# A new hand-written order for a retention and feed-forward kernel on one core: which engine does each step, when transfers are issued, and 42 waits between GpSimd and VectorE

## The chip, the core and the metric

The kernel runs on one core of a Trainium2 chip. The core has five engines with a queue each: TensorE (PE, matrix products), VectorE (DVE), ScalarE (ACT), GpSimd (POOL) and SyncE (SP), which here only issues transfers. Sixteen DMA engines serve the core. The metric is the device time of one execution in microseconds; lower is better. Every engine works through its own queue in order, and waits on semaphores for the others.

## What is computed

First a decayed attention for 8 batches of 8 heads over 576 positions of 64 numbers, then a feed-forward layer on all 4608 rows:

```python
Dmat = np.where(rel >= 0, gamma[:, None, None] ** rel[None, :, :], 0.0)   # rel[i, j] = i - j
ret = (scale * q @ k.T) * Dmat ; attn = ret @ v
x = attn.transpose(0, 2, 1, 3).reshape(4608, 512)
h = x @ w_in                    # 512 -> 2048
s = np.sin(alpha * h)
g = h + s * s / (alpha + 1e-09)
out = g @ w_out                 # 2048 -> 512
```

## The kernel before

The work is cut into nine groups of 512 rows. Groups 0 to 7 are the first 512 positions of a batch each, and group 8 holds the last 64 positions of all eight batches. Each small piece of work is a *step* with a name such as `PR.3.14.2`: a kind, the group or batch, and indices. The order of all steps is written out by hand in one long string, `STEPS`, with 1491 entries. At the end of the function a loop reads the entries from first to last and emits each as instructions; what stands earlier in the string stands earlier in the queue of its engine. An entry can say four things:

```
CA.3.q.1.2:G q16.3.1=12 <SQ.1.13
```

The step is the scaling of a raw block of q of batch 3; `:G` puts it on GpSimd (A is ScalarE, V VectorE, G GpSimd, P TensorE); `q16.3.1=12` places its result in the 12th of the buffers of that kind; `<SQ.1.13` makes it wait for the end of another step that it does not need any data from. Buffers are numbered slots: 8 banks of PSUM, 16 of 4 KB (`r4`), 28 of 2 KB (`h2`), 16 of 1 KB (`s1`). A step that writes a slot waits for those that still read it. There is no other scheduler.

The kinds of steps that the text speaks of, with the lines of the profile:

- LD (L431, L435): SyncE loads a raw block of q, k or v of 512 KB, two per tensor and batch, into an `r4` slot. LE does the same for the last 64 positions (L656). WI and WO load the weights from GpSimd's queue.
- CA (L458, copies of v L335): scales a raw block and converts it to 16 bits. XP (L490) turns blocks by a DMA transpose; for batches 0 and 1, TU (L476, TensorE) and TK (L335, copy) do.
- OU (L509), EV, TS (L335), MA (L534), MB (L537), NS (L542), ST (L548): the chain of the decayed k·v state. Of these only OU runs on TensorE.
- SC (L561, TensorE), MK (L574, VectorE): scores and their mask. VA, VB (L592) and SA (L628) apply them, KP copies the result into x.
- PR (L779, TensorE): a block of h in a PSUM bank. SI (L787, ScalarE): its sine. SQ (L797 on ScalarE, L798 on VectorE or GpSimd): the square. PD (L802, VectorE): g from square and bank, after which the bank is free.
- G2 (L818) multiplies g of group 0 by w_out; FI copies the result, OS stores it. Groups 1 to 8 use seven products instead of eight: TT (L854) forms differences of w_out once, SM (L866) sums and differences of g, PP (L886) the products on TensorE, CP (L335) copies and AD (L907) additions of results, OQ (L913, L914) the stores, mostly from SyncE's queue.
- KB (L422): products of zeros that keep TensorE busy while data is awaited at the start.

Two of the engines have a special relation in this kernel: the waits written with `<` stand on GpSimd steps only, each for a VectorE step beside it (35 of them before).

Of the kernel before, what the change touches and what calls it, by code (L numbers as in the profile page):

```python
# [34 lines left out]
KB.2.256.3; MA.0.2:V s32.0.2=17; RL.0.1:G; WI.1; TK.1.q.1.2:A qT.1.1=18; VB.0.1; MB.0.2:V; KB.8.256.7
ST.0.2:G <MB.0.2; ST.0.1:V; WI.3; SA.0.1; PR.0.2.0 hps.0.2=5; LD.1.k.1 raw.1.k.1=12; WO.0; KP.0.1.0:V; KP.0.1.1:A
KB.2.256.7; PR.0.2.1; CA.1.k.0.2:V k16.1.0=19; PR.0.0.2 hps.0.0=0; SI.0.2 s.0.2=0; LD.1.v.1 raw.1.v.1=13
CA.1.q.0.2:G q16.1.0=20; NS.0.3; PR.0.9.0 hps.0.9=1; PR.0.1.2 hps.0.1=2; SQ.0.2:V ss.0.2=1; PR.0.8.0 hps.0.8=3
SI.0.1 s.0.1=2; WO.1; PR.0.3.2 hps.0.3=4; SI.0.0 s.0.0=3; WO.2; PR.0.9.1; SQ.0.1:A ss.0.1=4; PR.0.11.2 hps.0.11=6
# [928 lines left out]
```

## Time and profile before

| | us |
|---|---|
| three runs | 300.96, 300.7, 303.81 |
| their median | 300.96 |
| the profiled execution | 300.28 |
| its span on the core | 298.4 |
| TensorE busy in it | 288.1 |

The profile is of one execution. Busy times are of its span, and the 1.9 us between span and time lie around it. Busy time of TensorE has modelled ends, so that short pauses between matmuls do not show as idle. The name L802 is line 802 of the kernel before; the changed kernel is one line shorter, so that the same line is L801 there. Names such as `r`, `h`, `s` and `g` in the rows are the buffers `r4`, `h2`, `s1` and `g16`.

### The profile page before, as it was taken

The numbers are of one execution on the slowest core, as the hardware profiler recorded it, in microseconds if no ns is written. First come the engines' busy times: TensorE is split into PE (matmuls) and PEld (weight loads), VectorE is DVE, ScalarE is ACT, GpSimd is POOL, SyncE is SP. The second block draws the span as 40 slices with busy tenths as digits, with TensorE's granted clock in tenths as the row PEclk, the third lists the DMA queues.
The fourth block names the chain that finished last, engine by engine and source line by source line (L and its number), as shares of the span: only waits on it lengthen the run. The fifth ranks groups of instructions, "written<-read, shape, count | busy, mean of one in ns | idle before, by whom it ended". The sixth has DMA issues, their size and how long they took to land.

```text
span 298.4 us, 8737 instructions
## 1 busy us (share of the span) xinstructions
PE 288.1 (97%) x3625; PEld 185.5 (62%) x3625; DVE 249.3 (84%) x369; ACT 191.2 (64%) x306; POOL 174.8 (59%) x161
## 2 busy tenths in 40 slices
PE   8999999998999999999999999999999999999994
PEld 4665445554666656667765667667665666465883
DVE  2567899999999899988989989879889766998931
ACT  1645952788756777597638864774677576877510
POOL 6745965389773865983794749974525543004380
PEclk9999999999999999999999999999999999999999
DMA  7999999999999999877977574167645000671054
GB/s 225 319 249 236 216 219 314 303 229 237 194 238 251 196 177 248 194 165 148 237 223 158 134 165 111 32 109 179 105 108 126 0 2 0 168 183 40 2 133 115
DMA packets 119511, 49.89 MB, mean 167 GB/s; under 512 B 69792, under 2 KB 118960, under 8 KB 119472
## 3 DMA queue, kind: packets, MB, share of 16 engines
...
## 4 chain that ended last, share of the span: by engine, by line
PE 73%; DVE 8%; DMA 6%; POOL 5%; SPq 4%; issue 2%; ACT 1%; DVEq 0%; ACTq 0%; POOLq 0%
PE banks L779 34%; PE banks L886 27%; DMA r<-in_q_dram 4%; DVE g L802 4%; PE banks L818 4%; SPq L435 4%; PE banks L561 2%; PE banks L592 2%; POOL s L798 2%; POOL r L866 2%; PE banks L509 1%; DMA r<-in_k_dram 1%; DVE h L574 1%; PE banks L628 1%; POOL h L458 1%
## 5 line engine op out<-in xcount | busy, mean ns | idle before, releaser
L779 PE MATMUL banks<-r,w_in 128*128 128x512 f16 (+1 forms) x608 | 139.1, 368 | 1.8 <-DVE g L802 1.3
L787 ACT ACTIVATE s<-banks,alpha 128x512 f16<-128x512 f32 x144 | 95.3, 686 | 55.0 <-PE banks L779 50.8
L802 DVE SCALAR_TENSOR_TENSOR g<-s,inva,banks 128x512 f16<-128x512 f16 x144 | 102.4, 741 | 15.9 <-ACT s L797 8.4
L779 PEld LDWEIGHTS <-w_in 128*128 128x128 f16 x608 | 57.6, 98 | 54.2 <-issue 3.2
L886 PEld LDWEIGHTS <-g 128*128 128x128 f16 x640 | 61.8, 98 | 17.1 <-issue 0.2
L797 ACT ACTIVATE s<-s 128x512 f16<-128x512 f16 x85 | 51.6, 628 | 1.4
L886 PE MATMUL banks<-w_out,g 128*128 128x256 f16 x384 | 51.2, 273 | 0.1
L458 POOL TENSOR_TENSOR h<-r,cn 128x1024 f16<-128x1024 f32 (+1 forms) x26 | 42.3, 1633 | 15.0 <-DVE s L798 5.9
L866 POOL TENSOR_TENSOR r<-g 128x1024 f16<-128x1024 f16 x10 | 21.6, 2162 | 37.0 <-DVE g L802 18.9
L798 POOL TENSOR_TENSOR s<-s 128x512 f16<-128x512 f16 x23 | 25.3, 1102 | 23.9 <-ACT s L787 19.8
L574 DVE TENSOR_TENSOR h<-banks,mask 128x1024 f16<-128x1024 f32 (+1 forms) x32 | 35.1, 1113 | 2.5 <-PE banks L561 2.4
L335 ACT COPY h<-banks 128x512 f32<-128x512 f32 (+2 forms) x32 | 20.8, 650 | 24.5 <-PE banks L886 17.8
L886 PE MATMUL banks<-r,g 128*128 128x256 f16 x256 | 34.8, 273 | 0.0
L886 PEld LDWEIGHTS <-r 128*128 128x128 f16 x256 | 24.5, 98 | 6.4 <-POOL r L866 0.5
L907 DVE TENSOR_TENSOR h<-banks,h 128x512 f32<-128x512 f32 (+1 forms) x26 | 16.7, 645 | 10.4 <-PE banks L886 8.2
L866 POOL TENSOR_TENSOR g<-g,r 128x1024 f16<-128x1024 f16 x8 | 17.4, 2183 | 12.6 <-DVE r L866 6.7
L335 ACT CAST r<-banks 128x1024 f16<-128x1024 f32 (+1 forms) x16 | 14.8, 932 | 10.7 <-PE banks L592 8.2
L798 DVE TENSOR_TENSOR s<-s 128x512 f16<-128x512 f16 x36 | 17.8, 499 | 4.3 <-ACT s L787 3.4
L458 DVE TENSOR_TENSOR h<-r,cn 128x512 f16<-128x512 f32 (+1 forms) x14 | 16.4, 1184 | 5.0 <-DMA r<-in_k_dram 4.2
L866 DVE TENSOR_TENSOR r<-g 128x1024 f16<-128x1024 f16 x22 | 16.6, 759 | 0.1
L886 PE MATMUL banks<-w_out,r 128*128 128x256 f16 x128 | 16.4, 273 | 0.0
L886 PE MATMUL banks<-r 128*128 128x256 f16 x128 | 16.2, 273 | 0.2 <-POOL r L866 0.2
...
## 6 DMA issues: line engine op xcount, KB each, us to landing
...
```

Of the source, the lines that this page charges most:

```text
L335: return eng.copy(d_, s_) if eng is nc.scalar else eng.tensor_copy(d_, s_)
L435: return eng.dma_start(t_, src[nm][b, :, 256 * p : 256 * p + 256, :].rearrange("h (i r) d -> i h (r d)", r=2))
L458: return eng.tensor_tensor(dst[:, a0:a1].rearrange("p a r t d -> p t (a r) d"), t_.rearrange("p (t a) x -> p t a x", t=2)[:, :, a0:a1].rea ...
L574: return nc.vector.tensor_tensor(ret(b, p, y).rearrange("p t (z x) -> p (t z) x", z=2)[:, :, 0:n], bank(f"sc.{b}.{p}.{y}", 2).rearrange("p ...
L779: i = matmul(bank(hps)[:, cols], w_in16[:, a, u * P : (u + 1) * P], x_of(n)[:, a, cols], start=starts(hps), stop=(a == KT - 1), skip_group ...
L787: return nc.scalar.activation(small(f"s.{name}")[:, cols], bank(f"hps.{name}")[:, cols], mybir.ActivationFunctionType.Sin, bias=0.0, scale ...
L797: return nc.scalar.activation(ss_t, s_t, mybir.ActivationFunctionType.Square)
L798: return eng.tensor_tensor(ss_t, s_t, s_t, MULT)
L802: return nc.vector.scalar_tensor_tensor(g_of(n)[:, u, cols], small(f"ss.{name}")[:, cols], inva[:, u : u + 1], bank(f"hps.{name}")[:, cols ...
L866: return eng.tensor_tensor(S[s], a, b, op)
L886: i = matmul(bank(f"{rows[c]}.{n}")[:, 256 * c : 256 * c + 256], left[:, 0, 128 * c : 128 * c + 128], right[:, 0, :], start=starts(f"{rows ...
L907: return nc.vector.tensor_tensor(x, bank(f"{b}.{n}")[:, cols], x, ADD)
```

## The change

The string `STEPS` is replaced by another with 1487 entries; no other line differs. The first nine entries are the same. The mix of steps is the same but for the warm-up products KB (19712 columns before, 20224 after) and a few steps that are cut or joined differently. Three things change: the order in every queue, the engine of about a hundred steps, and the waits with `<` (25 of the 35 are gone or changed, 32 are new or changed, 42 in all). Many slots change with them. The engines by kind, as ScalarE/VectorE/GpSimd:

| kind | before | after |
|---|---|---|
| SQ | 85/36/23 | 75/38/31 |
| CP | 22/10/0 | 27/5/0 |
| SM | 0/40/24 | 0/43/21 |
| CA | 12/14/33 | 14/15/30 |
| CE | 1/2/9 | 2/3/7 |
| MB | 0/6/16 | 0/4/18 |

In SyncE's queue the first fifteen loads keep their order; from then on single loads and transposes change places (LD.2.q.1 now ahead of LD.2.v.0, LD.3.k.1 ahead of LD.3.k.0), and the stores OQ of the second half are shuffled, with OQ.8.22, OQ.8.21 and the two halves of OQ.8.12 still the last. A few lines of the string, around the steps that the prediction speaks of (cut):

```diff
-LD.4.k.0 raw.4.k.0=10; SI.1.13 s.1.13=5; G2.0.2.1 op.0.2=3; CA.2.v.0.2:A v16.2.0=14; TT.4.1:V T4=12; G2.0.2.3
-SQ.1.13:V ss.1.13=6; LD.3.k.1 raw.3.k.1=11; SI.1.3 s.1.3=1; PD.1.13 gT.1=1; CA.3.q.1.2:G q16.3.1=12 <SQ.1.13; G2.0.0.2
...
-CA.2.k.1.0:G; G2.0.2.0; SI.1.7 s.1.7=7; FI.0.1:V osb.0.1=17; TT.4.0:V; PR.1.9.2 hps.1.9=5; SQ.1.7:A ss.1.7=3
...
+PR.1.3.2 hps.1.3=2; CA.2.v.0.2:V v16.2.0=14; G2.0.0.2; TT.4.1:V T4=12; SI.1.3 s.1.3=1; FI.0.1:V osb.0.1=17
+SQ.1.6:A ss.1.6=2; G2.0.2.1; LD.4.k.0 raw.4.k.0=10; CA.3.q.1.2:G q16.3.1=12; CA.2.v.1.2:A v16.2.1=15; PD.1.6 gT.1=1
...
+G2.0.0.3; SQ.1.5:V ss.1.5=10; SQ.1.7:A ss.1.7=3; CA.2.k.1.0:G <TT.4.0; PD.1.7; G2.0.2.0; FI.0.0:A osb.0.0=20
```

The first place is VectorE's queue in batch 1, before. The rows are, from the top, CA.2.q.1.2, TT.4.1, SQ.1.13, PD.1.13, PD.1.6, SQ.1.5, FI.0.1, TT.4.0, PD.1.7, PD.1.5, PD.1.3 and EV.2.0; the names are buffers, and the brackets hold the engines and transfers that are waited for.

```order
L458 TENSOR_TENSOR h_68<-r_67,cn 128x2x8x64 [waits DMAHW3_49]
L854 TENSOR_TENSOR r_67<-w_out_65,r_67 128x1024 [waits DMAHW5_49,DVE_49]
L798 TENSOR_TENSOR s_69<-s_69 128x512 [waits Activation_49]
L802 SCALAR_TENSOR_TENSOR g_70<-s_69,inva,banks 128x512 [waits DVE_49,PE_49]
L802 SCALAR_TENSOR_TENSOR g_70<-s_69,inva,banks 128x512
L798 TENSOR_TENSOR s_69<-s_69 128x512 [waits Activation_49]
L335 COPY h_68<-banks 128x512
L854 TENSOR_TENSOR r_67<-w_out_65,r_67 128x1024
L802 SCALAR_TENSOR_TENSOR g_70<-s_69,inva,banks 128x512 [waits Activation_49]
L802 SCALAR_TENSOR_TENSOR g_70<-s_69,inva,banks 128x512 [waits DVE_49]
L802 SCALAR_TENSOR_TENSOR g_70<-s_69,inva,banks 128x512 [waits Pool_49]
L335 COPY r_67<-banks 128x512 [waits DMAHW6_49,PE_49]
```

The same stretch of VectorE's queue in the change: TT.2.0, CA.2.v.0.2, TT.4.1, FI.0.1, PD.1.6, PD.1.13, TT.4.0, SQ.1.5, PD.1.7, PD.1.3, PD.1.5, EV.2.0.

```order
L853 TENSOR_TENSOR r_67<-w_out_65,r_67 128x1024 [waits DMASW6_49,DVE_49]
L334 CAST h_68<-r_67 128x1024 [waits DMAHW3_49]
L853 TENSOR_TENSOR r_67<-w_out_65,r_67 128x1024 [waits DMAHW5_49]
L334 COPY h_68<-banks 128x512 [waits PE_49]
L801 SCALAR_TENSOR_TENSOR g_70<-s_69,inva,banks 128x512 [waits Activation_49]
L801 SCALAR_TENSOR_TENSOR g_70<-s_69,inva,banks 128x512 [waits DVE_49,PE_49]
L853 TENSOR_TENSOR r_67<-w_out_65,r_67 128x1024 [waits DVE_49]
L797 TENSOR_TENSOR s_69<-s_69 128x512 [waits Activation_49]
L801 SCALAR_TENSOR_TENSOR g_70<-s_69,inva,banks 128x512 [waits Activation_49]
L801 SCALAR_TENSOR_TENSOR g_70<-s_69,inva,banks 128x512 [waits Pool_49]
L801 SCALAR_TENSOR_TENSOR g_70<-s_69,inva,banks 128x512 [waits DVE_49,PE_49]
L334 COPY r_67<-banks 128x512 [waits DMAHW6_49,PE_49]
```

The cast CA.2.v.0.2 has come over from ScalarE and stands ahead of TT.4.1, and PD.1.3, the row that waits for GpSimd, has changed places with PD.1.5. ST.1.3, TT.1.0 and SQ.1.13 now stand a few rows ahead of this piece; TT.1.1 and TT.2.1 have come before TT.1.0 and TT.2.0.

The second place is GpSimd's queue beside it, before: CA.2.k.1.1, CA.2.q.0.2, CA.3.q.1.2, CA.2.k.1.0, SQ.1.3, CA.3.k.0.0, SQ.1.4.

```order
L458 TENSOR_TENSOR h_68<-r_67,cn 128x2x4x64 [waits DMAHW7_49,PE_49]
L458 TENSOR_TENSOR h_68<-r_67,cn 128x2x8x64 [waits PE_49,DMAHW0_49,DVE_49]
L458 TENSOR_TENSOR h_68<-r_67,cn 128x2x8x64 [waits DMAHW5_49,DVE_49,PE_49]
L458 TENSOR_TENSOR h_68<-r_67,cn 128x2x4x64
L798 TENSOR_TENSOR s_69<-s_69 128x512 [waits DVE_49,Activation_49]
L458 TENSOR_TENSOR h_68<-r_67,cn 128x2x4x64 [waits DMAHW6_49,PE_49]
L798 TENSOR_TENSOR s_69<-s_69 128x512 [waits Activation_49,Pool_49]
```

The same seven steps in the change:

```order
L457 TENSOR_TENSOR h_68<-r_67,cn 128x2x4x64 [waits DMAHW7_49,PE_49]
L457 TENSOR_TENSOR h_68<-r_67,cn 128x2x8x64 [waits DMAHW0_49,DVE_49]
L457 TENSOR_TENSOR h_68<-r_67,cn 128x2x8x64 [waits DMAHW5_49,PE_49]
L457 TENSOR_TENSOR h_68<-r_67,cn 128x2x4x64 [waits DVE_49]
L797 TENSOR_TENSOR s_69<-s_69 128x512 [waits Activation_49]
L457 TENSOR_TENSOR h_68<-r_67,cn 128x2x4x64 [waits DMAHW7_49,PE_49]
L797 TENSOR_TENSOR s_69<-s_69 128x512 [waits Activation_49]
```

The order is the same; the waits for VectorE (DVE) have moved: CA.3.q.1.2 has lost its wait for SQ.1.13, and the wait for TT.4.0 that stood on SQ.1.3 now stands one row earlier, on CA.2.k.1.0. A little later in this queue MB.2.1 has a new wait for TT.3.1, ST.2.1 for SM.1.3.1 and CA.3.k.1.0 for TT.3.0.

More of the change, by code (lines that the diff above doesn't have):

```diff
@@ L35 @@
[L35 to L39, printed above, removed]
@@ new lines @@
+WO.1; PD.0.2 gT.0=0; WO.2; PR.0.3.2 hps.0.3=4; SI.0.1 s.0.1=2; SI.0.9 s.0.9=14; TU.1.q.0.2 tr.1.q.0=7
+SQ.0.1:V ss.0.1=4; ST.0.3:V; PR.0.11.2 hps.0.11=6; SQ.0.0:V ss.0.0=5; PD.0.1; PR.0.5.2 hps.0.5=5; SI.0.11 s.0.11=6
+TK.1.q.0.1:V qT.1.0=21; TK.1.q.0.0:V; SI.0.8 s.0.8=7; PR.0.4.2 hps.0.4=2; SQ.0.11:G ss.0.11=9; PD.0.0
+PR.0.6.2 hps.0.6=7; SI.0.4 s.0.4=11; SQ.0.8:G ss.0.8=10; PD.0.11; LD.2.k.1 raw.2.k.1=14; SI.0.5 s.0.5=15
+PR.0.7.2 hps.0.7=0; SQ.0.4:G ss.0.4=12; PD.0.8; SI.0.3 s.0.3=8; SQ.0.5:V ss.0.5=2; SQ.0.3:A ss.0.3=0
@@ new lines @@
+SM.1.3.1:V S3.1=15; PR.1.0.0 hps.1.0=0; ST.2.0:G s16.2=27; SQ.1.11:A ss.1.11=2; SC.2.0.1 sc.2.0.1=6; SQ.1.8:A ss.1.8=5
+LE.0.k rs.0.k=23; PR.1.0.1; MK.2.0.1 ret.2.0.1=21; SI.1.2 s.1.2=7; ST.2.1:G <SM.1.3.1; G2.0.2.2; SQ.1.10:A ss.1.10=6
+MA.2.2:G s32.2.2=2; PD.1.8; SI.1.0 s.1.0=4; XP.2.q.1 qT.2.1=22; CA.3.k.0.1:G; SC.2.0.0 sc.2.0.0=6
+MK.2.0.0 ret.2.0.0=26; PR.1.1.2 hps.1.1=2; CA.3.q.0.2:G q16.3.0=25; PD.1.10; VA.2.0 o.2.0=6; XP.3.q.1 qT.3.1=4
+TT.3.0:V; RL.2.0:A; SI.1.1 s.1.1=3; SA.2.0; PR.1.12.2 hps.1.12=5; SQ.1.1:A ss.1.1=1; PD.1.11
@@ new lines @@
+SI.2.11 s.2.11=6; LE.2.q rs.1.q=16; PP.1.6.1; PD.2.3 gT.2=0; SI.2.7 s.2.7=3; ST.3.0:G s16.3=26 <SM.1.2.1; PP.1.6.2
+LD.4.v.1 raw.4.v.1=0; SQ.2.11:V ss.2.11=4; PP.1.6.3; MA.3.2:G s32.3.2=21; SQ.2.7:A ss.2.7=2; PD.2.11
+PR.2.2.2 hps.2.2=1; CP.1.6:A u2.1=13; LD.4.k.1 raw.4.k.1=9; SM.1.4.1:G <SQ.2.11; PD.2.7; PP.1.5.2 Z.1=3
+SI.2.2 s.2.2=7; LD.6.k.0 raw.6.k.0=2; CA.4.k.0.2:V k16.4.0=2; SC.3.1.1 sc.3.1.1=4; PP.1.5.0; PP.1.5.3
+SC.3.1.0 sc.3.1.0=6; PR.2.1.2 hps.2.1=0; MK.3.1.0 ret.3.1.0=19; MB.3.2:G <CA.4.k.0.2; PP.1.7.3; SI.2.1 s.2.1=1
@@ new lines @@
+SM.3.3.1:G <SM.3.3.0; SQ.3.13:A ss.3.13=12; PD.3.13; RL.4.0:P; PP.3.1.0; SI.3.11 s.3.11=8; SA.4.0
+OU.5.2 kv.5.0=1 kv.5.1=4; SQ.3.11:A ss.3.11=11; VB.4.0; PP.2.3.1; EV.5.0:A kvs.5=4; PD.3.11; XP.5.k.0 kT.5.0=4
+PP.3.1.2; KP.4.0.2:A x.4=9; PP.3.2.0 Y.3=1; SM.3.1.0:V; PR.3.15.2 hps.3.15=2; EV.5.1:A; MA.5.1:V s32.5.1=8
+XP.5.k.1 kT.5.1=11; SM.3.2.0:V S2.3=5; MB.5.1:G; VA.4.1 o.4.1=6; SI.3.15 s.3.15=13; PP.3.1.3; CA.6.v.1.2:A v16.6.1=2
+PP.3.2.1; SQ.3.15:V ss.3.15=14; OQ.1.22; RL.4.1:P; PD.3.15; MA.5.2:G s32.5.2=12 <SQ.3.15; SA.4.1; VB.4.1
```

374 lines of the change are left out of this document (179 added, 195 removed).

## The prediction

> **What bounds the kernel now.** First view: the page's engine totals, then its forty slices, where each digit is the busy share of a slice of 7.5 us in tenths.
>
> ```profile
> PE 288.1 (97%) x3625; PEld 185.5 (62%) x3625; DVE 249.3 (84%) x369; ACT 191.2 (64%) x306; POOL 174.8 (59%) x161
> PE   8999999998999999999999999999999999999994
> DVE  2567899999999899988989989879889766998931
> PEclk9999999999999999999999999999999999999999
> DMA  7999999999999999877977574167645000671054
> ```
>
> TensorE is busy 97% of the span at full granted clock; VectorE is full beside it from about the fifth slice to the fifteenth (30 to 115 us), and the DMA engines nearly so from the start to that point. A change of order leaves TensorE's work as it is, so the question is how much of the time it stands still, and where. Second view: the busy times cut by stretches (columns: length, then busy time and count of PE, PEld, DVE, ACT, POOL, the clock, the DMA share, GB/s).
>
> ```profile
> 0.00:20.00 20.00, 17.93 (x311) 11.98 (x311) 10.74 (x18) 9.24 (x13) 12.25 (x24) 1.00 1.04 258
> 20.00:32.00 12.00, 11.58 (x86) 6.37 (x85) 8.07 (x14) 6.80 (x12) 8.52 (x10) 1.00 1.19 248
> 32.00:49.00 17.00, 15.97 (x260) 8.71 (x259) 16.23 (x28) 10.30 (x17) 12.40 (x14) 1.00 1.18 245
> 49.00:57.00 8.00, 8.00 (x77) 4.58 (x75) 7.97 (x10) 3.81 (x6) 2.02 (x1) 1.00 1.02 303
> 57.00:67.00 10.00, 10.00 (x125) 4.85 (x123) 9.50 (x15) 8.84 (x15) 8.42 (x8) 1.00 1.07 245
> 67.00:77.00 10.00, 8.71 (x127) 4.71 (x124) 9.84 (x12) 8.54 (x16) 9.48 (x9) 1.00 1.10 220
> 77.00:120.00 43.00, 42.89 (x606) 27.88 (x603) 41.61 (x58) 30.16 (x50) 28.03 (x27) 1.00 1.00 219
> 120.00:200.00 80.00, 79.57 (x1095) 53.28 (x1094) 71.11 (x104) 57.52 (x91) 58.61 (x49) 1.00 0.66 151
> 200.00:285.00 85.00, 84.64 (x882) 55.75 (x881) 71.98 (x111) 54.23 (x88) 30.48 (x23) 1.00 0.37 84
> ```
>
> Length minus the first number is TensorE's idle time. From 77 to 285 us it is 0.11 + 0.43 + 0.36 = 0.9 us in 208: no order of the other engines can win more than that there. Between 20 and 77 us it is 0.42 + 1.03 + 0 + 0 + 1.29 = 2.74 us. That, with a part of the 2.07 us before 20 us, is all that is to be had; a loss has no such ceiling. Third view: what those idle stretches wait for, in the timeline of TensorE (in brackets the idle time before a row and who ended it).
>
> ```profile
> 38.49 0.45 PE L509 MATMUL banks<-h 64*64 64x64 f16 x32 [0.29 <-DVE g L802]
> 39.42 0.41 PE L561 MATMUL banks<-h 64*64 64x128 f16 x15 [0.43 <-ACT r L335]
> 69.09 1.02 PE L779 MATMUL banks<-r,w_in 128*128 128x512 f16 x4 [0.24 <-DVE g L802]
> 70.88 1.02 PE L779 MATMUL banks<-r,w_in 128*128 128x512 f16 x4 [0.24 <-DVE g L802]
> 73.03 1.02 PE L779 MATMUL banks<-r,w_in 128*128 128x512 f16 x4 [0.66 <-DVE g L802]
> ```
>
> Twice it waits near 39 us (OU.1.0 for a bank that PD empties, SC for TS) and three times between 69 and 73 us, for PD on VectorE (L802) to empty a bank for the next PR. VectorE itself is busy 9.84 of 10 us there and 7.97 of 8 us from 49 on: **from 49 to 73 us VectorE sets the pace, and what its queue gains or loses by 73 us is what TensorE gains or loses.** After that TensorE carries any shift unchanged to the end.
>
> **The change part by part.**
>
> *Lead-in, to 32 us.* The first fourteen transfers keep their order; the warm-up matmuls grow from 19712 to 20224 columns. At the rate of the chain of waits, four matmuls of 512 columns in 0.86 us, the 512 columns more are 0.2 us; they stand where TensorE waits for data anyway (2.07 us idle before 20 us). I take 0; the bounds are 0 and +0.2.
>
> *32 to 49 us.* OU.1.0 moves into a bank that is free sooner, and TS.1.0 to VectorE, so the 0.29 and 0.43 us above go, and VectorE loses four small steps here (TK.1.k.1.1, SQ.0.13, MB.1.1, MA.1.2, 0.42 us each by two rows below). TensorE then comes some 0.7 us earlier to 49 us, VectorE up to as much. As VectorE is the pace from there, TensorE's own lead ends as more waiting at 69 to 73 us. I count it at 0 (bounds −0.7 and 0), and VectorE's in the next part.
>
> *VectorE from 49 us to EV.2.0* (the first two order pieces). VectorE and GpSimd in the timeline, then lines grouped by shape:
>
> ```profile
> 49.49 2.39 DVE L854 TENSOR_TENSOR r<-w_out 128x1024 f16<-128x1024 f16 x1
> 52.94 0.68 DVE L854 TENSOR_TENSOR r<-w_out,r 128x1024 f16<-128x1024 f16 x1
> 58.72 0.67 DVE L798 TENSOR_TENSOR s<-s 128x512 f16<-128x512 f16 x1 [0.16 <-ACT s L787]
> 59.91 0.93 DVE L854 TENSOR_TENSOR r<-w_out,r 128x1024 f16<-128x1024 f16 x1
> 62.88 0.68 DVE L335 COPY r<-banks 128x512 f32<-128x512 f32 x1
> 65.85 1.01 DVE L866 TENSOR_TENSOR r<-g 128x1024 f16<-128x1024 f16 x1
> 70.74 1.57 DVE L854 TENSOR_TENSOR w_out<-w_out 128x1024 f16<-128x1024 f16 x1
> ```
> ```profile
> 49.31 2.02 POOL L458 TENSOR_TENSOR h<-r,cn 128x1024 f16<-128x1024 f32 x1 [0.74 <-DVE h L548]
> 57.21 3.08 POOL L458 TENSOR_TENSOR h<-r,cn 128x1024 f16<-128x1024 f32 x2 [5.88 <-DVE s L798]
> 60.98 1.04 POOL L798 TENSOR_TENSOR s<-s 128x512 f16<-128x512 f16 x1 [0.69 <-ACT s L797]
> ```
> ```profile
> L534 DVE TENSOR_TENSOR h<-r,cn 128x256 f32<-128x256 f32 x10 | 4.2, 417 | 0.0
> L335 DVE CAST r<-banks 128x1024 f16<-128x1024 f32 x1 | 1.2, 1217 | 0.0
> L335 DVE CAST s<-h 128x512 f16<-128x512 f32 x1 | 0.9, 860 | 0.0
> L335 DVE COPY h<-banks 128x512 f16<-128x512 f16 x4 | 1.6, 418 | 0.1
> ```
>
> The first VectorE row is a meeting: TT.1.0 took 2.39 us where the same shape takes 0.68, and ended 0.55 us after CA.2.q.0.2 on GpSimd had (49.31 + 2.02 = 51.33). A step with two inputs in SBUF that starts during such a GpSimd step stands until that ends, and then runs. So 1.71 us are lost here, 0.25 at 58.72 (0.67 for 0.42), 0.25 at 59.91, 0.33 at 65.85, 0.89 at 70.74. In the new order CA.2.q.0.2 still waits for ST.1.2, and TT.1.1 follows that in VectorE's queue, so the first meeting stays. Its GpSimd step was released by ST.1.2 (the 0.74 in its row), not by data, so with VectorE's lead it may begin up to 0.7 us sooner; I take −0.7, bounds −0.7 and 0. Then, up to EV.2.0, VectorE has two steps more: ST.1.3 (0.42), which stood before the meeting, and CA.2.v.0.2, on ScalarE before. That cast from SBUF on VectorE is in no row: between 0.42, a 16-bit copy of half the size, and 1.72, twice the cast of 128x512, I take 1.2, the one VectorE cast of its shape, from PSUM. So −0.7 + 0.42 + 1.2 = +0.9.
>
> The Trainium skill, "VectorE: DVE Perf Modes", section "The perf-mode tier table (the rule you actually need)", lets a single-input 32-bit copy between SBUF tiles make two results a cycle, which would give an estimate of about 0.7 us for this cast and +0.4 for the sum; no run here shows it.
>
> Next the new wait: CA.2.k.1.0 may start only after TT.4.0. That removes the stretches at 58.72 and 59.91 (−0.5). But behind it in GpSimd's queue stands SQ.1.3, and PD.1.3 on VectorE waits for that. TT.4.0 ends near 60.3, the cast takes (3.08 less the 1.9 of its full-sized neighbour) 1.2 us, SQ.1.3 1.04 us: 62.6, where VectorE would be at PD.1.3 at 61.3. That is +1.3 at most, where PD.1.5, which stood ahead of it, now stands behind; bounds 0 and +1.3, and I take +0.8, as the wait shrinks where VectorE itself comes later. So EV.2.0 ends 0.9 − 0.5 + 0.8 = 1.2 us later than the 63.56 of before.
>
> *64 to 73 us.* VectorE's order here is the same in both. ST.2.1 now waits for SM.1.3.1 and MB.2.1 for TT.3.1, which frees SM.1.3.1 of its 0.33; CA.3.k.1.0 waits for TT.3.0, which should win half of its 0.89. VectorE also stood 0.3 us before MK at 67 us, which absorbs that much. So −0.33 − 0.4 − 0.3 = −1.0, and at 73 us VectorE, and with it TensorE, is 0.2 us later.
>
> *CA.3.q.1.2 without its wait.* SyncE's issues of LD.2.q.1 and LD.3.q.1, and the answer for that line:
>
> ```profile
> 46.96 1.35 SPq L435 DMA_DIRECT2D r<-in_q_dram  x1
> 50.40 1.32 SPq L435 DMA_DIRECT2D r<-in_q_dram  x1
> DMA to landing us min/median/max: 4.9/6.7/21.9
> ```
>
> LD.2.q.1 and LD.2.v.0 change places in that queue, one issue (1.4 us) apart; LD.2.v.0 lands at about 46.96 + 6.7 = 53.7, and VectorE reaches its cast near 56, so this costs nothing. LD.3.q.1 keeps its place and lands at about 50.40 + 6.7 = 57.1. Before, CA.3.q.1.2 waited for SQ.1.13 and began at 57.21. Now it begins on landing, and TT.4.1, at 56.00 before, stands behind the new cast and comes at about 57.1 too. If GpSimd is first, TT.4.1 is stuck for nearly the 1.9 us of such a step: +1.8. If VectorE is first, 0. I take 0, slightly the likelier, since a faster cast than 1.2 would bring VectorE there sooner.
>
> *77 to 285 us.* About a hundred steps change engine: SQ goes from ScalarE/VectorE/GpSimd 85/36/23 to 75/38/31, CP from 22/10/0 to 27/5/0, SM from 0/40/24 to 0/43/21. Ten SQ less on ScalarE and eight more on GpSimd, with the rest, moves each engine's total by under 1.5 us by the mean of each group, and TensorE idles 0.9 us here. 0, bounds −0.5 and +0.7.
>
> *Tail.* Two rows:
>
> ```profile
> 285.54 1.05 PE L886 MATMUL banks<-r 128*128 128x256 f16 x8 [0.24 <-POOL r L866]
> 292.91 0.60 SPq L913 DMA_DIRECT2D out_dram<-h  x1
> ```
>
> The product of SM.8.2.1 waits 0.24 us for GpSimd; the new order puts one product more between, so this may go. SyncE's queue has its stores in another order, but OQ.8.21 and OQ.8.12 stay its last. Nine pairs now stand from OQ.7.22 to OQ.8.22, 9 × 2 × 0.6 = 11 us, after a sum that ends some 15 us before TensorE does, by TensorE's rows: they just fit. I take −0.2, bounds −0.4 and +1.
>
> **Sum.** Lead-in 0, TensorE's lead 0, VectorE +1.2 − 1.0, the lost wait 0, from 77 us 0, tail −0.2: 0 on the profiled execution's 300.28 us. The runs shown have a median of 300.96, 0.7 more. I forecast **300.8 us** for the median.
>
> **The rivals.**
> 1. *GpSimd first at 57 us.* As above, +1.8: 302.6. For it: the cast of VectorE in front of TT.4.1 at its row price. Against it: the 0.7 by which the stretch may begin sooner.
> 2. *The meetings go and the lead stays.* If TensorE's 0.7 us survive and the meetings between 49 and 73 us (1.71 + 0.25 + 0.25 + 0.33 + 0.89 = 3.4) shrink to a third, 0.7 + 2.3 = 3.0 us are won, which is about all of the idle time of 20 to 77 us and of the tail: 297.8. For it: GpSimd now waits beside four of these five. Against it: the largest, beside CA.2.q.0.2, waited just so before. The Trainium skill, "SBUF — State Buffer", section "Who interferes with whom", states that a two-input VectorE step and a GpSimd step that reads SBUF lock each other out, for the whole of the one that started first. By that rule a wait moves a meeting's whole loss to GpSimd; the trace agrees as far as TT.1.0 ends 0.55 us after the GpSimd step.
> 3. *Slower: GpSimd falls behind.* Its queue holds eight SQ more and seven waits more.
>
> ```profile
> L802 DVE SCALAR_TENSOR_TENSOR g<-s,inva,banks 128x512 f16<-128x512 f16 x144 | 102.4, 741 | 15.9 <-ACT s L797 8.4 <-POOL s L798 5.9 <-PE banks L592 0.6
> L798 POOL TENSOR_TENSOR s<-s 128x512 f16<-128x512 f16 x23 | 25.3, 1102 | 23.9 <-ACT s L787 19.8 <-DVE s L798 2.7 <-ACT s L797 0.7
> ```
>
> PD already waits 5.9 us for the 23 SQ of GpSimd, 0.26 us each. Eight more at that price are 2.1 us, and 8.8 if each waits for a whole SQ (1.10 us); at half a microsecond each they are 4.0: 304.8. It costs time from the point where a PD ends later than TensorE comes back to its bank, first between 77 and 120 us, where VectorE is busy 41.61 of 43 us and can't catch up. Against it: GpSimd is busy only 28.03 us there.
> 4. *The waits do nothing*: then the 0.5 and 0.7 us credited to them stay lost, 302.0, inside the first rival's span.
>
> **How the numbers follow.** The likeliest case (299.8 to 301.6) has 0.42, the first rival (to 303.5) 0.25, the second 0.14, the third 0.19. A measurement here can tell about 1%, 3.0 us, from no change. Half of the third rival's chance lies above 304.2 and under half of the second's below 297.6, which leave out some 0.17: the range is **297.6 to 304.2**. Faster by over 1% takes nearly all of the second: 0.13; slower by over 1% the third with a little of the first: 0.20; the rest, 0.67, is within.
>
> **What would show it.** In the profile after: the rows near 39 us without their 0.29 and 0.43; still a two-input L853 step of over 2 us at about 49 us; the PE rows at 69 to 75 us with as much idle time as before, again ended by VectorE's PD; TT.4.1 near 57 us at 0.68 (or 2.5 in the first rival); PD.1.3 near 62 us waiting for GpSimd; TensorE's idle time from 77 to 285 us near 0.9. The prediction is wrong if TensorE idles where it now is full, say over 2 us between 77 and 285, if its stretch from 67 to 77 us idles under 0.3 us, or if the stores end more than 5 us after its last matmul.

## The result, and the profile after

| | before | after |
|---|---|---|
| median of twenty runs each, us | 302.06 | 304.14 |
| profiled execution, us | 300.28 | 303.69 |
| its span, us | 298.4 | 302.0 |

The ratio is 1.0068, with a 95% interval of 1.004 to 1.0095: the change makes the kernel slower by 0.7%, some 2.1 us. The prediction was no change (300.8 us, or 0.9995 of the median shown then). As a time, 304.14 us still lies just inside the range of 297.6 to 304.2, but not because the working was right: over twenty runs the kernel before is itself 1.1 us above the base of the forecast, and 1.0068 of that base, 300.96 us, is 303.0 us, the time of the first rival. Two of the twenty executions after, of 308.07 and 1641.43 us, are over 1.5% above the fastest and don't count in the ratio. The kernel before varied from 299.8 to 305.5 us over these runs, so times are compared by ratios, and profiles serve only to see where time goes. A ratio here is the figure on record with its interval; it isn't the quotient of the two medians, and differs from that by up to 0.23%.

The first view to compare is the cut by stretches, after:

```profile
0.00:20.00 20.00, 17.31 (x309) 12.03 (x310) 9.71 (x15) 9.16 (x12) 14.13 (x26) 1.00 1.03 257
20.00:32.00 12.00, 11.43 (x87) 6.40 (x84) 9.89 (x18) 6.21 (x10) 8.26 (x9) 1.00 1.19 249
32.00:49.00 17.00, 16.17 (x244) 8.86 (x244) 15.23 (x23) 11.37 (x20) 11.63 (x13) 1.00 1.18 244
49.00:57.00 8.00, 8.00 (x91) 4.64 (x90) 7.95 (x13) 2.87 (x4) 2.60 (x2) 1.00 1.08 322
57.00:67.00 10.00, 8.71 (x102) 4.04 (x100) 8.81 (x13) 7.48 (x12) 5.39 (x5) 1.00 1.08 254
67.00:77.00 10.00, 8.48 (x119) 4.27 (x118) 9.46 (x14) 7.80 (x14) 8.42 (x9) 1.00 0.61 153
77.00:120.00 43.00, 42.32 (x611) 27.12 (x609) 41.44 (x58) 30.87 (x52) 28.25 (x27) 1.00 0.98 212
120.00:200.00 80.00, 79.63 (x1096) 52.87 (x1090) 70.30 (x100) 57.20 (x91) 56.65 (x47) 1.00 0.69 155
200.00:285.00 85.00, 84.63 (x873) 55.01 (x872) 72.44 (x110) 56.37 (x92) 36.14 (x28) 1.00 0.38 80
```

Length less the first number is again TensorE's idle time. From 57 to 285 us it is 1.29 + 1.52 + 0.68 + 0.37 + 0.37 = 4.23 us, where it was 0 + 1.29 + 0.11 + 0.43 + 0.36 = 2.19 before: 2.04 us more. That this is also the difference of the medians is in part chance, as the two profiled executions differ by 3.4 us: to the last matmul TensorE idles 2.4 us more and is busy 1.1 us longer (289.15 against 288.06), and where that busy time comes from the profiles don't show. Two stretches make most of the 2.04: 57 to 67 us, where TensorE had been full, gains 1.29, and 77 to 120 us gains 0.57. Ahead of 57 us idle time also shifts (2.69 + 0.57 + 0.83 instead of 2.07 + 0.42 + 1.03), but there the warm-up products fill gaps, and by the matmuls of the trace TensorE has done the same real work by 57 us in both, to 0.2 us.

What happens at 57 us, in the timelines of VectorE, GpSimd and TensorE after:

```profile
55.78 0.68 DVE L853 TENSOR_TENSOR r<-w_out,r 128x1024 f16<-128x1024 f16 x1
56.39 2.39 DVE L334 CAST h<-r 128x1024 f16<-128x1024 f32 x1
58.70 0.68 DVE L853 TENSOR_TENSOR r<-w_out,r 128x1024 f16<-128x1024 f16 x1
59.30 0.68 DVE L334 COPY h<-banks 128x512 f32<-128x512 f32 x1
64.17 1.41 DVE L801 SCALAR_TENSOR_TENSOR g<-s,inva,banks 128x512 f16<-128x512 f16 x2 [0.94 <-POOL s L797]
```
```profile
56.30 1.93 POOL L457 TENSOR_TENSOR h<-r,cn 128x1024 f16<-128x1024 f32 x1 [5.35 <-DMA r<-in_q_dram]
61.97 1.16 POOL L457 TENSOR_TENSOR h<-r,cn 128x512 f16<-128x512 f32 x1 [3.74 <-DVE r L853]
```
```profile
60.03 1.89 PE L778 MATMUL banks<-r,w_in 128*128 128x512 f16 x8 [1.29 <-DVE h L334]
68.48 0.60 PE L778 MATMUL banks<-r,w_in 128*128 128x256 f16 x4 [0.57 <-DVE g L801]
```

CA.3.q.1.2 on GpSimd no longer waits for SQ.1.13; its idle time is ended by the transfer (5.35 <-DMA), at 56.30. The cast CA.2.v.0.2, new on VectorE, starts 0.09 us after it and takes 2.39 us: it ends 0.55 us after the GpSimd step does (56.30 + 1.93 = 58.23). FI.0.1, the copy that empties the bank for the next PR, stands two places behind it, and TensorE waits 1.29 us for it. The last rows of the first and third fence are the second loss foreseen: GpSimd waits with CA.2.k.1.0 for TT.4.0 (3.74), SQ.1.3 comes behind it, PD.1.3 waits 0.94 us and TensorE 0.57.

### The profile page after: what moved, and what is told of

Read it like the earlier page. It is cut to its first block, busy times and chain, and to the rows that moved or that the text cites. A ratio compares the mean times of both kernels' runs of the same rounds, so it can differ in the third digit from the quotient of the medians.

```text
span 302.0 us, 8737 instructions
## 1 busy us (share of the span) xinstructions
PE 289.1 (96%) x3625; PEld 186.1 (62%) x3625; DVE 250.9 (83%) x367; ACT 191.7 (63%) x306; POOL 173.6 (57%) x163
## 4 chain that ended last, share of the span: by engine, by line
PE 70%; DVE 8%; DMA 7%; SPq 4%; issue 3%; POOL 3%; ACT 3%; DVEq 0%; POOLq 0%; ACTq 0%
PE banks L778 32%; PE banks L885 28%; DVE g L801 3%; DVE h L573 2%; PE banks L591 2%; PE banks L560 2%; DMA r<-in_v_dram 2%; DMA r<-in_q_dram 2%; DMA r<-in_k_dram 2%; PE banks L508 2%; PE banks L817 1%; POOL s L797 1%; DMA s<-s 1%; SPq L434 1%; PE banks L627 1%
## 5 line engine op out<-in xcount | busy, mean ns | idle before, releaser
L801 DVE SCALAR_TENSOR_TENSOR g<-s,inva,banks 128x512 f16<-128x512 f16 x144 | 102.3, 740 | 14.2 <-ACT s L796 8.2
L457 POOL TENSOR_TENSOR h<-r,cn 128x1024 f16<-128x1024 f32 (+1 forms) x26 | 43.6, 1683 | 22.9 <-DMA r<-in_q_dram 9.3
L334 ACT COPY h<-banks 128x512 f32<-128x512 f32 (+2 forms) x37 | 23.7, 641 | 38.1 <-PE banks L885 26.7
L797 POOL TENSOR_TENSOR s<-s 128x512 f16<-128x512 f16 x31 | 32.1, 1041 | 27.1 <-ACT s L786 23.5
L796 ACT ACTIVATE s<-s 128x512 f16<-128x512 f16 x75 | 46.4, 629 | 1.7 <-DMA s<-s 0.3
L885 PE MATMUL banks<-r,g 128*128 128x256 f16 x256 | 35.7, 273 | 0.0
L797 DVE TENSOR_TENSOR s<-s 128x512 f16<-128x512 f16 x38 | 22.1, 583 | 5.6 <-ACT s L786 5.4
L536 POOL TENSOR_TENSOR r<-h,r 128x256 f32<-128x256 f32 x18 | 13.2, 732 | 19.6 <-DVE r L865 8.9
L334 ACT CAST r<-banks 128x1024 f16<-128x1024 f32 (+1 forms) x18 | 15.9, 895 | 5.9 <-PE banks L627 3.1
L457 DVE TENSOR_TENSOR h<-r,cn 128x512 f16<-128x512 f32 (+1 forms) x14 | 14.6, 1055 | 4.5 <-DMA r<-in_k_dram 3.7
L885 PE MATMUL banks<-w_out,r 128*128 128x256 f16 x128 | 15.9, 272 | 0.0
```

Of the source, the lines that this page charges most:

```text
L334: return eng.copy(d_, s_) if eng is nc.scalar else eng.tensor_copy(d_, s_)
L457: return eng.tensor_tensor(dst[:, a0:a1].rearrange("p a r t d -> p t (a r) d"), t_.rearrange("p (t a) x -> p t a x", t=2)[:, :, a0:a1].rea ...
L536: return eng.tensor_tensor(sum_of(b, c), s32(b, c), sum_of(b, c), ADD)
L796: return nc.scalar.activation(ss_t, s_t, mybir.ActivationFunctionType.Square)
L797: return eng.tensor_tensor(ss_t, s_t, s_t, MULT)
L801: return nc.vector.scalar_tensor_tensor(g_of(n)[:, u, cols], small(f"ss.{name}")[:, cols], inva[:, u : u + 1], bank(f"hps.{name}")[:, cols ...
```

## The experiments

Theory A: the change loses because it dropped the wait of CA.3.q.1.2, so that this GpSimd step and VectorE meet at 57 us (a *meeting* is a GpSimd step and a VectorE step from SBUF that overlap, one of them stretched). Theory B: the cast is simply dear on VectorE. Later, theories on the other waits and on what is left. All times are in five rounds beside the kernel before, whose medians in these sets were 301.5 to 302.0 us.

### The dropped wait put back

The new wait is for TT.4.1, the last of the VectorE steps from SBUF at this place; SQ.1.13, which the old wait named, now stands ahead of them.

```diff
-CA.3.q.1.2:G q16.3.1=12
+CA.3.q.1.2:G q16.3.1=12 <TT.4.1
```

> One wait more than the change: CA.3.q.1.2 on GpSimd waits for TT.4.1 on VectorE. Theory A (the loss at 57 us is the meeting of the cast CA.2.v.0.2 on VectorE with CA.3.q.1.2 on GpSimd): the cast falls from 2.39 us to 0.7 to 1.2, FI.0.1 ends over 1 us earlier, TensorE's wait of 1.29 us before PR at 60 us falls below 0.3, and the ratio to before falls from 1.007 to about 1.003. Theory B (a cast of this shape from SBUF costs 2.4 us on VectorE by itself): the cast stays at 2.4, and so do the wait and the ratio (1.007).

Measured: 302.85 us, ratio 1.0047 (1.0017 to 1.0077). VectorE, GpSimd and TensorE in its timeline:

```profile
56.24 0.69 DVE L334 CAST h<-r 128x1024 f16<-128x1024 f32 x1
62.48 1.41 DVE L801 SCALAR_TENSOR_TENSOR g<-s,inva,banks 128x512 f16<-128x512 f16 x2 [0.76 <-POOL s L797]
```
```profile
57.66 1.90 POOL L457 TENSOR_TENSOR h<-r,cn 128x1024 f16<-128x1024 f32 x1 [6.76 <-DVE r L853]
```
```profile
58.43 1.89 PE L778 MATMUL banks<-r,w_in 128*128 128x512 f16 x8
66.79 0.60 PE L778 MATMUL banks<-r,w_in 128*128 128x256 f16 x4 [0.54 <-DVE g L801]
```

With nothing of GpSimd beside it the cast takes 0.69 us, and the PR that came at 60.03 comes at 58.43 without a wait. Theory B falls. By its ratio the gain is 0.2%, and the interval overlaps that of the change. But the six kernels of the new order with this wait, this one and five below, have medians of 302.3 to 302.9 us, and the five without it (the change in two sets, and three edited ones below) 303.7 to 304.3. In each of the three sets that hold both sorts, run side by side, those with the wait are 0.95 to 1.7 us quicker; by the ratios the two groups nearly part (1.0013 to 1.0047 and 1.0042 to 1.0086).

### The cast back on ScalarE

```diff
-CA.2.v.0.2:V v16.2.0=14
+CA.2.v.0.2:A v16.2.0=14
```

> Only the engine of CA.2.v.0.2 goes back, from VectorE to ScalarE. Theory A (whatever VectorE step from SBUF stands beside CA.3.q.1.2 is stuck): the cast takes 1.04 us on ScalarE, but TT.4.1, now at about 56.4, is stuck beside CA.3.q.1.2 for about 2 us, and the ratio stays between 1.004 and 1.007. Theory B (the price of the cast on VectorE): the loss goes, ratio 1.002 or less.

Measured: 303.8 us, 1.0067 (1.0037 to 1.0098), as expected of theory A, but the profile does not show why. In it the transfer was issued and landed 0.8 us later than in the change, and TT.4.1 (in one row with TT.2.0) got ahead of the GpSimd step, whose row is 2.21 us long instead of 1.9. VectorE, GpSimd and TensorE:

```profile
56.30 1.29 DVE L853 TENSOR_TENSOR r<-w_out,r 128x1024 f16<-128x1024 f16 x2
```
```profile
57.14 2.21 POOL L457 TENSOR_TENSOR h<-r,cn 128x1024 f16<-128x1024 f32 x1 [6.03 <-DMA r<-in_q_dram]
```
```profile
59.10 1.89 PE L778 MATMUL banks<-r,w_in 128*128 128x512 f16 x8
```

TensorE lost nothing at 57 us in that execution: the last VectorE step from SBUF was already under way, and the next, FI.0.1, reads a bank. It idled more elsewhere (1.15 us from 120 to 200 us, 0.37 in the change). For A and B this run is inconclusive, since one profile without the loss stands beside a median like the change's; it shows that under a microsecond in the landing decides who is first.

### The old order with the cast on VectorE

```diff
-CA.2.v.0.2:A v16.2.0=14
+CA.2.v.0.2:V v16.2.0=14
```

> The kernel before with one engine changed: the cast CA.2.v.0.2 on VectorE, as in the change. There CA.3.q.1.2 still waits for SQ.1.13, so nothing of GpSimd runs beside the cast. Theory A: it takes 0.69 us, TT.4.1 and what follows are 0.6 us later, and TensorE's waits at 69 to 73 us grow by up to that: ratio 1.000 to 1.003. If the engine alone were the loss (theory B): 1.005.

Measured: 303.23 us, 1.004 (1.0006 to 1.0074). The cast, alone beside a waiting GpSimd, takes 0.69 us again; TensorE does not wait at 58 us, and idles less at 67 to 77 us than before, not more:

```profile
56.10 0.69 DVE L335 CAST h<-r 128x1024 f16<-128x1024 f32 x1
```
```profile
57.00:67.00 10.00, 10.00 (x116) 4.77 (x118) 9.86 (x16) 7.86 (x14) 7.92 (x8) 1.00 1.09 246
67.00:77.00 10.00, 9.42 (x144) 5.27 (x144) 9.93 (x13) 9.09 (x17) 9.92 (x9) 1.00 0.96 202
120.00:200.00 80.00, 78.29 (x1082) 52.09 (x1080) 69.26 (x100) 55.95 (x90) 57.67 (x48) 1.00 0.70 153
```

Its ratio lies between theory A's 1.003 and theory B's 1.005, with both inside the interval, and is not explained by this place: in the profile its loss lies at 120 to 200 us (1.71 us idle), a stage that is taken up below.

### The old order without that one wait

```diff
-CA.3.q.1.2:G q16.3.1=12 <SQ.1.13
+CA.3.q.1.2:G q16.3.1=12
```

> The kernel before with one wait less: CA.3.q.1.2 no longer waits for SQ.1.13, the one wait of this place that the change drops. Theory A (that wait held this stage together): CA.3.q.1.2 starts when its data lands, near 56.3 us, SQ.1.13 stands beside it for about 2 us, TensorE waits some 1.0 us before PR at 59.7 us, and the ratio is 1.003 to 1.005. Theory J (the 35 waits only work together, and the loss without all of them comes from elsewhere): ratio 0.999 to 1.002.

Measured: 302.46 us, 1.002 (0.9993 to 1.0046). The mechanism is there as expected, with another VectorE step in the place of the cast. SQ.1.13 on VectorE before, then in this kernel, and TensorE:

```profile
56.62 0.42 DVE L798 TENSOR_TENSOR s<-s 128x512 f16<-128x512 f16 x1
```
```profile
56.83 2.11 DVE L798 TENSOR_TENSOR s<-s 128x512 f16<-128x512 f16 x1
```
```profile
59.84 1.02 PE L779 MATMUL banks<-r,w_in 128*128 128x512 f16 x4 [1.06 <-DVE g L802]
```

SQ.1.13, 0.42 us before, takes 2.11, and TensorE waits 1.06 us where it did not wait at all. Nearly all of that is still there at 77 us: TensorE idles 2.27 us from 57 to 77 us, against 1.29 before. The rows are theory A's, but the ratio is theory J's, and does not separate this kernel from the one before. So in these profiles the wait is worth a microsecond of TensorE at its place, in both orders, and by the time alone only the new order shows it.

### All waits taken out, in either order; and one put back

The same edit in every entry with a wait, 42 in the new order and 35 in the old; the third kernel keeps the wait of the first experiment.

```diff
-CA.2.q.0.2:G q16.2.0=6 <ST.1.2
+CA.2.q.0.2:G q16.2.0=6
...
```

> The change without its 42 waits of GpSimd for VectorE; order and engines stay. Theory E (the new order is the loss, the waits save some of it): more stretched VectorE steps than with them, ratio to before 1.010 or more. Theory F (the waits themselves cost the time, as GpSimd's late steps are waited for): ratio 1.003 or less. Theory G (a wait only decides which of the two loses the time): 1.005 to 1.009, as with the waits (1.007).

> The kernel before without its 35 waits. Theory E: ratio 1.003 or more. Theory G: 0.998 to 1.003.

> The change without its 42 waits, but with the one of the first experiment, CA.3.q.1.2 for TT.4.1. Theory G (a wait mostly decides which engine loses the time, and this one is the exception since GpSimd is idle behind it): the cast on VectorE at 0.69 us, TensorE without its 1.3 us wait at 58 us, and a ratio below 1.0042 (that of no waits at all), 0.999 to 1.003. Theory E (the 42 are worth something): 1.004 to 1.008.

Measured: the change without its waits 303.68 us, 1.0042 (1.0007 to 1.0078); with the one wait for TT.4.1 alone 302.83 us, 1.0038 (1.0002 to 1.0074); the kernel before without its waits 303.95 us, 1.0054 (1.0023 to 1.0085). In the new order the 41 other waits are worth nothing that can be measured (1.0038 without them, 1.0047 with). That is what theory G says, though 1.0042 lies between its figures and theory F's, with both inside the interval; the one wait shows by its profile (0.69 us for the cast) and not by the ratio against no waits at all. In the old order the 35 are worth some 0.5% (0.2 to 0.9): theory E. VectorE in the new order without waits:

```profile
56.24 0.69 DVE L334 CAST h<-r 128x1024 f16<-128x1024 f32 x1
56.84 2.39 DVE L853 TENSOR_TENSOR r<-w_out,r 128x1024 f16<-128x1024 f16 x1
```

Here VectorE came to the cast 0.15 us sooner, just ahead of GpSimd's step (56.27). The cast was first and free, and TT.4.1 behind it was stuck instead; TensorE waited the same 1.29 us, at 59.89. So it does not matter which of the two is caught.

Why a wait may be worth nothing is seen at another place, SM.3.4.1 (the GpSimd rows below), which in the change got a wait for CA.6.k.1.2 (the first VectorE row of each pair; the second is PD.4.2). First the rows before (VectorE, GpSimd), then after:

```profile
145.84 3.17 DVE L458 TENSOR_TENSOR h<-r,cn 128x1024 f16<-128x1024 f32 x1
149.94 0.75 DVE L802 SCALAR_TENSOR_TENSOR g<-s,inva,banks 128x512 f16<-128x512 f16 x1 [0.93 <-POOL s L798]
```
```profile
145.81 2.12 POOL L866 TENSOR_TENSOR g<-g,r 128x1024 f16<-128x1024 f16 x1
```
```profile
148.94 1.40 DVE L457 TENSOR_TENSOR h<-r,cn 128x1024 f16<-128x1024 f32 x1
153.67 0.75 DVE L801 SCALAR_TENSOR_TENSOR g<-s,inva,banks 128x512 f16<-128x512 f16 x1 [2.46 <-POOL s L797]
```
```profile
150.52 2.12 POOL L865 TENSOR_TENSOR g<-g,r 128x1024 f16<-128x1024 f16 x1 [1.25 <-DVE h L457]
```

The wait frees CA.6.k.1.2 (3.17 to 1.40 us) and delays SM.3.4.1 by 1.25; SQ.4.2 stands behind that on GpSimd, and PD.4.2 on VectorE waits for it 2.46 us instead of 0.93. VectorE gained 1.77 us and gave 1.53 back two rows on.

### The meeting at 89 us

```diff
-SM.1.4.1:G <SQ.2.11
...
+CA.4.k.0.2:V k16.4.0=2; SM.1.4.1:G <CA.4.k.0.2
```

> SM.1.4.1 on GpSimd waits for CA.4.k.0.2 on VectorE instead of SQ.2.11. Theory A (a second loss near 93 us is the meeting of these two): CA.4.k.0.2 falls from 2.21 us to 1.2, the wait of 0.59 us of TensorE before SC near 93 us goes, ratio about 1.004 to 1.005. Theory C (GpSimd is late here, so that a wait of 2 us more in its queue only moves the loss to MB.3.2, ST.3.2 and what follows): the ratio stays at 1.007 or grows.

> Both edits, of CA.3.q.1.2 and of SM.1.4.1. Theory A for both: the gains add up to some 2 us and the ratio comes to about 1.000 (0.998 to 1.003). If the two losses are only where TensorE's slack happens to show and other waits take their place (theory D), the ratio stays above 1.004.

Measured: alone 304.3 us, 1.0086 (1.0056 to 1.0115); with the wait of the first experiment 302.85 us, 1.0041 (1.0014 to 1.0068). The step CA.4.k.0.2 on VectorE before; then VectorE and TensorE after, and in the first of these kernels:

```profile
86.47 1.64 DVE L458 TENSOR_TENSOR h<-r,cn 128x1024 f16<-128x1024 f32 x1
```
```profile
89.00 2.21 DVE L457 TENSOR_TENSOR h<-r,cn 128x1024 f16<-128x1024 f32 x1
93.52 0.42 PE L560 MATMUL banks<-h 64*64 64x128 f16 x16 [0.59 <-DVE h L573]
```
```profile
89.07 1.22 DVE L457 TENSOR_TENSOR h<-r,cn 128x1024 f16<-128x1024 f32 x1
93.29 0.42 PE L560 MATMUL banks<-h 64*64 64x128 f16 x16 [0.27 <-DVE h L573]
```

The step is freed and half of TensorE's wait goes, 0.3 us, but the time doesn't fall. That is theory C's side, and for the two edits together (1.0041, above 1.004) barely theory D's. What is gained at this place is too small to see in the time; whether it comes back behind isn't shown.

### The late SQ.1.3

```diff
-CA.2.k.1.0:G <TT.4.0
-SQ.1.3:G ss.1.3=11
+CA.2.k.1.0:G
+SQ.1.3:G ss.1.3=11 <TT.4.0
```

This kernel too has the wait for TT.4.1.

> The first experiment (CA.3.q.1.2 waits for TT.4.1) and, as in the order before, the wait for TT.4.0 on SQ.1.3 instead of CA.2.k.1.0. Theory H (the wait on CA.2.k.1.0 makes SQ.1.3 late, PD.1.3 waits for it, and so PR near 67 us): PD.1.3's wait of 0.76 us and TensorE's of 0.54 near 67 us go, ratio some 0.0015 below the first experiment's 1.0047. Rival: CA.2.k.1.0 then runs beside TT.4.0, which is stuck for 0.3 to 1.2 us, and the ratio stays at 1.0047.

Measured: 302.31 us, 1.0013 (0.9989 to 1.0038). The ratio is the lowest of all kernels in the new order, on theory H's side, but by the profile nothing is gained at this place, as the rival says. VectorE and TensorE:

```profile
60.26 1.27 DVE L797 TENSOR_TENSOR s<-s 128x512 f16<-128x512 f16 x1
62.46 1.41 DVE L801 SCALAR_TENSOR_TENSOR g<-s,inva,banks 128x512 f16<-128x512 f16 x2 [0.27 <-POOL s L797]
```
```profile
66.77 0.60 PE L778 MATMUL banks<-r,w_in 128*128 128x256 f16 x4 [0.28 <-DVE g L801]
```

PD.1.3 waits 0.27 instead of 0.76 us, and SQ.1.5 is stuck beside CA.2.k.1.0 (1.27 for 0.42), so that PD.1.3 starts at 62.46 against 62.48 and the PR behind it at 66.77 against 66.79. The kernel with the one wait alone has the same rows here, and a ratio of 1.0038. The profiled executions took 302.17 and 302.34 us. The intervals overlap (0.9989 to 1.0038 and 1.0017 to 1.0077), and the lower ratio is not taken for a gain.

### Work moved from GpSimd to VectorE

```diff
-SM.1.1.0:G
-SM.1.4.1:G <SQ.2.11
-SQ.1.3:G ss.1.3=11
+SM.1.1.0:V
+SM.1.4.1:V
+SQ.1.3:V ss.1.3=11
```

Both kernels move the two SM and have the wait for TT.4.1; only the second moves SQ.1.3.

> The first experiment, with SM.1.1.0 and SM.1.4.1 moved from GpSimd to VectorE. Theory I (on GpSimd these 2.1 us steps cost VectorE 0.9 and 1.0 us by keeping SM.1.1.1 and CA.4.k.0.2 stuck, more than the 0.7 us that each takes on VectorE itself): no stretched step at 81 and 87 us, TensorE's wait of 0.59 us near 92 us at most 0.3, ratio 0.001 to 0.003 below the first experiment's 1.0047. Rival: VectorE is full here, its 1.4 us more make PD and MK late by as much as the stretches did, ratio unchanged.

> The change with CA.3.q.1.2 waiting for TT.4.1, SM.1.1.0 and SM.1.4.1 on VectorE, and SQ.1.3 on VectorE too. Theory K (what is left of the loss after the first wait is PD.1.3 waiting for GpSimd's SQ.1.3, then PR): PD.1.3 doesn't wait, TensorE's wait of 0.54 us near 67 us goes, and the ratio is 1.000 to 1.002 instead of 1.003. Rival: VectorE has 0.42 us more to do and is as late: 1.003.

Measured: 302.46 us, 1.003 (1.000 to 1.006), and 302.92 us, 1.0035 (1.0008 to 1.0062). In the first VectorE does more and is busy less; the stretch from 77 to 120 us, first of the wait alone and then with the two SM moved:

```profile
77.00:120.00 43.00, 42.31 (x602) 27.47 (x599) 41.40 (x58) 30.77 (x52) 28.16 (x25) 1.00 0.99 213
```
```profile
77.00:120.00 43.00, 42.63 (x609) 27.83 (x602) 40.94 (x60) 31.15 (x52) 24.44 (x23) 1.00 0.98 212
```

VectorE has 60 steps instead of 58 and 40.94 us of busy time instead of 41.40; TensorE idles 0.37 instead of 0.69 us. The direction is that of theory I; its size can't be told from the time. In the second, SQ.1.3 on VectorE took 1.10 us beside CA.2.k.1.0, and TensorE's 0.57 us at 67 us stayed: the rival.

### A wait of the change in the old order

```diff
-CA.3.k.1.0:G k16.3.1=1
+CA.3.k.1.0:G k16.3.1=1 <TT.3.0
```

> The kernel before with one wait of the change added: CA.3.k.1.0 on GpSimd waits for TT.3.0. TT.3.0 falls from 1.57 us to 0.7, PD.1.11 comes 0.8 us sooner, and TensorE's wait of 0.66 us before PR at 73 us goes: ratio 0.998. Rival (theory G): CA.3.k.1.0 is then later by 0.7 us, and MB.2.2, ST.2.2 and SA with it, ratio 1.000 to 1.002.

Measured: 302.03 us, 1.002 (0.9982 to 1.0058); no gain, as the rival has it. At its place the wait does what it should. VectorE and TensorE:

```profile
70.98 0.68 DVE L854 TENSOR_TENSOR w_out<-w_out 128x1024 f16<-128x1024 f16 x1
129.00 0.43 DVE L534 TENSOR_TENSOR h<-r,cn 128x256 f32<-128x256 f32 x1 [1.81 <-DMA h<-h]
```
```profile
72.53 1.04 PE L779 MATMUL banks<-r,w_in 128*128 128x512 f16 x4
141.75 0.37 PE L561 MATMUL banks<-h 64*64 64x128 f16 x16 [1.21 <-DMA h<-h]
```
```profile
120.00:200.00 80.00, 76.62 (x1070) 50.82 (x1069) 67.55 (x99) 54.33 (x87) 55.81 (x46) 1.00 0.70 154
```

TT.3.0 falls from 1.57 to 0.68 us and the wait of 0.66 us at 73 us is gone. Then, from 120 to 200 us, TensorE idles 3.38 us instead of 0.43, and two of its waits there, on VectorE and TensorE, are for DMA transposes. The profiled executions of the old order idle there 0.43, 1.15 (no waits), 1.54 (one wait less), 1.71 (cast on VectorE) and 3.38 us; those of the new order 0.37 to 1.20, but 2.72 with the one wait alone and 3.69 without waits, in executions of 304.7 and 306.7 us, 1.9 and 3.0 above their medians. So this stage differs by some 3 us between profiled executions, more than any effect looked for here, and a single profile can't explain a ratio of a few tenths of a per cent. Whether the edits or the executions make the difference isn't shown; nor is it that transfers which land just in time or not are behind it, which the two rows suggest. No kernel of this study beats the one before.

### The change again

> The changed kernel again, beside the others. If the meeting of CA.2.v.0.2 with CA.3.q.1.2 comes in every run, its profile shows the cast at 2.4 us and a wait of TensorE of about 1.3 us at 58 us again, and the ratio is 1.004 to 1.009; if it hangs on when LD.3.q.1 happens to land, the cast may show 0.69 us.

Measured: 304.15 us, 1.0079 (1.0049 to 1.011). The profiled execution took 307.88 us, well above that median, so its times aren't compared; the order of its steps answers the question. VectorE (TT.2.0), GpSimd and TensorE:

```profile
59.48 2.39 DVE L853 TENSOR_TENSOR r<-w_out,r 128x1024 f16<-128x1024 f16 x1
```
```profile
58.81 2.51 POOL L457 TENSOR_TENSOR h<-r,cn 128x1024 f16<-128x1024 f32 x1 [4.52 <-DMA r<-in_q_dram]
```
```profile
63.73 1.89 PE L778 MATMUL banks<-r,w_in 128*128 128x512 f16 x8 [1.29 <-DVE h L334]
```

GpSimd came earlier against VectorE than in the first profile. TT.2.0, the step ahead of the cast, was caught, the cast took 0.68 us, and TensorE waited the same 1.29 us.

## Why the prediction was wrong

The step that failed is "CA.3.q.1.2 without its wait", put at 0 with +1.8 as a rival of chance 0.25. The rival came: TensorE lost 1.29 us there at once, from 57 to 67 us, where it had been full. The sign that I had given for the rival, TT.4.1 at 2.5 us, did not show (0.68 us), as the cast stood in its place. Three errors made 0 look the likelier:

- *The landing.* I took the median of 6.7 us from issue to landing, hence 57.1 us. In the profile before, this very transfer did take 6.7 us. In the change it took 5.9, and in the other profiles where it releases the GpSimd step 5.9 three times, 6.2 once, and 7.3 in the execution of 307.88 us. The step on GpSimd starts at 56.30, and at 56.27, 56.38, 56.69 and 57.14 in four of the others. What I left out is this spread, 0.8 us against VectorE steps that are 0.6 us apart. At 56.3 VectorE was still in TT.2.0, and whatever came next was caught.
- *The price of the cast.* 1.2 us was taken from a cast that reads PSUM. Alone it is 0.69 us, the 0.7 estimated from the Trainium skill, "VectorE: DVE Perf Modes", section "The perf-mode tier table (the rule you actually need)". That would have made the sum 0.5 us better, and was no help against the meeting: where nothing catches it, TT.4.1 starts at 56.85 to 57.60 in the profiles with the wait, near the 57.1 that I reckoned.
- *What can be caught.* I named TT.4.1 as the step at risk, as one with two inputs in SBUF. The cast has one, and was caught for the whole of the GpSimd step. The Trainium skill, "SBUF — State Buffer", section "Who interferes with whom", says that a copy or cast that runs in a mode with both ports also takes the shared pair; the 2.39 us beside GpSimd and 0.69 without agree.

More deeply, I asked only who would be first at TT.4.1, and took 0 as slightly the likelier. VectorE's queue there is one SBUF step after another (TT.2.0, the cast, TT.4.1), and the profiles of the new order without the wait show what counts. Where the GpSimd step came while one of these was still to start, TensorE lost 1.29 us, whether TT.2.0, the cast or TT.4.1 was caught (four of five profiles). Where it came behind the start of the last of them, at 57.14 with the cast on ScalarE, TensorE lost nothing. So "if VectorE is first, 0" held for TT.4.1, but it needed a landing as late as the one before. For the landing that came, the term is +1.3 and not 0.

The other steps, by what the profile after shows:

- The *wait of PD.1.3*: 0.8 predicted, 0.94 measured. Right, and the edits meant to remove it only moved it. Summed up, EV.2.0 ends 2.6 us later than before (65.49 + 0.68 = 66.17 against 63.56), where 1.2 was forecast; with the wait of the first experiment it ends 0.9 later (63.80 + 0.68 = 64.48). So the rest of that part held, and the lost wait is what was missing.
- The *first meeting* stayed: TT.1.1 took 1.85 us at 49.65, a little under the 2 us that I gave as its sign. Right. SM.1.3.1 fell to 0.71 and TT.3.0 to 1.06 us, as reckoned (0.68 and about 1.17).
- *39 us*: the 0.29 us went, the 0.43 did not (TensorE waits 0.43 us for the TS that is now on VectorE). No effect, since the lead was counted at 0.
- *77 to 285 us*: 0 predicted; idle time went from 0.90 to 1.42 us, within the bound of +0.7. Nearly all of it is the wait of 0.59 us at 93.5 us. The meetings ahead of it, of SM.1.1.0 with SM.1.1.1 at 82 us and of SM.1.4.1 with CA.4.k.0.2 at 89 us, are in the profile before too, shorter (1.15 and 1.64 us against 1.63 and 2.21); I didn't look at them. Taking one or both away removed 0.3 us of the wait.
- *Rival 3*, the late GpSimd, did not come: in the group of all PD, the idle time ahead is 14.2 us, after 15.9 before, and GpSimd's part of it 4.9 after 5.9.

```profile
L801 DVE SCALAR_TENSOR_TENSOR g<-s,inva,banks 128x512 f16<-128x512 f16 x144 | 102.3, 740 | 14.2 <-ACT s L796 8.2 <-POOL s L797 4.9
```

- *The tail*: the last store was issued 298.38 us into a span of 302.0, TensorE's last row starts at 295.58; 0.24 us won, nothing lost.

So the sum should have been +1.3 for the caught VectorE steps and +0.5 for 77 to 120 us: about +1.8 on the same base, against 2.1 measured. The 300.8 was also low because the median of three runs, 300.96, was: over twenty it is 302.06. And the sum of 0 on that base gives 300.96 and not 300.8; the 0.16 us between has no term.

What stays open: with the wait back some 0.35% (1 us) is left. The profile of that kernel has 0.9 us more idle time from 57 to 285 us than before: 0.54 at 67 us and 0.58 between 77 and 120 us are new, and 0.34 from 67 to 77 us is saved. The edits at the causes named there gave ratios whose intervals all overlap its own, and at 67 us one wait took the place of another. Open too is why the kernel with the cast on ScalarE is as slow as the change, though its profile has no loss at 57 us. By the time alone, that the dropped wait costs anything in the old order isn't shown either.
